# Placing the gate, up and down products of two routed rows in an attention kernel's instruction order

## The chip, the cores and the metric

The kernel runs on one core of a Trainium2 chip. The metric is the device time of one execution in microseconds (us). TensorE (PE in the profile) multiplies matrices, VectorE (DVE), ScalarE (ACT) and GpSimd (POOL) work on elements, and SyncE (SP) issues most of the transfers. Each engine takes its instructions in the order in which they are written.

## The reference

```python
xn = layernorm(x)                       # x: 2048 rows of 640
# attention: 32 heads of 192, keys and values from the last 512 rows of the caches
q = xn @ wq;  p = softmax(q k^T * 192**-0.5);  s = concat(p v) @ wo
# routed part: the two rows with the highest r = xn @ w_r
x_sel = rows of xn at the two positions
y = (silu(x_sel @ w_gate) * (x_sel @ w_up)) @ w_down     # 640 -> 1536 -> 640
y = y * sigmoid(r at the two positions)
g = silu(xn + scatter(y to the two positions))
out = x + s * g
```

The attention is nearly all of the work. The routed part has two rows only, but its result is needed by g for these rows, and it runs inside the attention as a background job.

## The kernel before

**Units and stretches.** A unit n is 128 rows of queries of a pair of heads; there are 256. Units are worked on in stretches of three (the first two stretches have two units). Stretch j starts with the scores of its units and ends with the value products of the units of stretch j-1. From stretch 11 on the order within a stretch is built by a function, `stretch(j)`, as a list of tokens, and the tokens are emitted one after the other. Because the schedule is manual, the order of emission is the order on each engine.

**The order in a stretch** is: S (scores of three units, six matmuls over 128 rows of the contraction and six over the other 64), B.j.0 (background, slot 0), M (six row maxima on DVE, L332), E (exponentials on ACT, L339, two for each unit) with P (transposes of the probabilities on SP, L344) for the first two units, then q (query projections, L303, with their evacuations on ACT, L295), E and P of the third unit, B.j.1, W (output products, L406, evacuated by DVE, L420) with B.j.2 behind the first of them, O (value products of stretch j-1, L358, evacuated by DVE, L373), T (the transpose of their result, L379) and B.j.3. A stretch has two or three q and one or two W, by due times that a planner works out. In the stretches of interest these are: 31 (two q, two W), 36 (two q, one W), 41 (three q, one W) and 48 (two q, two W).

**PSUM.** There are two pools. `ps_p` has six buffers, for the scores (six in a stretch), the W tiles (two for each W) and the first two O tiles of a stretch. `ps_f` has two buffers, for q, for the third O tile, and for the background products `gu_ps` and `y_ps`.

**Background jobs** are put at a unit's stretch and a slot by

```python
def at(n, slot, f):
    bg[st_of[min(n, NU - 1)], slot].append(f)
```

and emitted when the token B.j.slot comes up. The ones of the routed part that matter here are:

- `m_ffn_piece(fb, q)`: ten transfers for each of three blocks fb of 512 columns, which load the gate and up weights into one tile `wgu` (a pool of one buffer, shared with the down weights `wd` and with `y_bc`).
- `m_mul(fb)`: twenty matmuls of the two rows (in 32 columns, in four column groups) with the gate and up weights into `gu_ps` (L576), a tanh on ACT (L580), and two steps on DVE (L581, L582) that give h.
- `m_hT(fb)`: a transpose of h by SP (L588).
- `m_wd_piece(q)`: six transfers of the down weights.
- `m_down`: 48 matmuls of the same kind into `y_ps` (L613), one step on DVE (L616), then five transfers from POOL that bring y to all partitions (L619, L621).
- `m_add(n)` on POOL (L625, L628, L629), which adds y to the routed rows, and `m_tanh(n)` on ACT (L634), which reads the sum.

Of the kernel before, what the change touches and what calls it, by code (L numbers as in the profile page):

```python
# [21 lines left out]
def kernel(ctx, tc, A_x, A_k_cache, A_v_cache, A_wq, A_wo, B_x, B_w_r, B_w_gate, B_w_up, B_w_down, out):  # L22
# [52 lines left out]
    def f_tile(shape, dtype, name):  # L75
        return ps_f.tile(shape, dtype, name=name, tag="f")
# [485 lines left out]
    def m_ffn_piece(fb, q):  # L562
        def f():
            if q == 0:
                M["wgu"] = M["w"].tile([P, 2, DC, 512], BF16, name="wgu", tag="w")
            w, dc = divmod(q, DC)
            src = (B_w_gate, B_w_up)[w].rearrange("(c p) f -> p c f", p=P)
            nc.sync.dma_start(out=M["wgu"][:, w, dc, :], in_=src[:, dc, fb * 512:(fb + 1) * 512])
        return f

    def m_mul(fb):
        def f():
            gu = f_tile([P, 2, P], FP32, "gu_ps")
            for dc in range(DC):
                for c in range(4):
                    nc.tensor.matmul(gu[32 * c:32 * c + 32], lhsT=M["xsT"][:, dc, 0:32], rhs=M["wgu"][:, :, dc, c * P:(c + 1) * P],  # L576
                                     start=(dc == 0), stop=(dc == DC - 1), skip_group_check=True)
            th = M["s"].tile([P, P], FP32, name="th", tag="t2")
            h = M["s"].tile([P, P], BF16, name="h", tag="turned")
            nc.scalar.activation(out=th, in_=gu[:, 0, :], func=ACT.Tanh, scale=0.5)  # L580
            nc.vector.scalar_tensor_tensor(out=th, in0=th, scalar=1.0, in1=gu[:, 0, :], op0=ALU.add, op1=ALU.mult)  # L581
            nc.vector.scalar_tensor_tensor(out=h, in0=th, scalar=0.5, in1=gu[:, 1, :], op0=ALU.mult, op1=ALU.mult)  # L582
            M["h"] = h
        return f

    def m_hT(fb):
        def f():
            nc.sync.dma_start_transpose(out=M["hT"][:, fb * 4:(fb + 1) * 4, :].rearrange("p c t -> p (c t)"), in_=M["h"])  # L588
        return f
# [149 lines left out]
    def at(n, slot, f):  # L739
        bg[st_of[min(n, NU - 1)], slot].append(f)  # L740

    for g in range(2, NG):
        n0 = 32 * g
# [25 lines left out]
    for fb, n0 in enumerate((72, 91, 106)):  # L769
        for q in range(2 * DC):  # L770
            at(n0 + q, 0, m_ffn_piece(fb, q))
        at(n0 + (16, 14, 14)[fb], 3, m_mul(fb))
        at(n0 + (16, 14, 14)[fb], 3, m_hT(fb))
    for q in range(FC // 2):
        at(121 + 3 * q, 0, m_wd_piece(q))
    at(124, 3, m_sig)
    at(141, 2, m_down)
    for n in range(NTB):
        at(147 + 2 * n, 3, m_add(n))
        at(186 + 2 * n, 0, lambda n=n: m_tanh(n))  # L780
# [131 lines left out]
```

## Time and profile before

| what | value |
|---|---|
| median of 3 runs | 792.39 us (791.88 to 793.05) |
| the profiled execution, its own time | 792.56 us |
| its span on the core | 790.8 us |
| granted TensorE clock | 1.00 |
| gate and up products, start | 279.97, 326.32 and 372.68 us |
| down product, start | 432.35 us |
| start of the scores of stretches 31, 36, 41, 48 | 280.63, 326.99, 373.34, 436.91 us |

The span is from the first to the last instruction of the core in one profiled execution, and the time of that execution is a little longer. Rows in order of time give the start and the length in us, the engine, the line, and what is written from what; equal instructions that follow each other are merged, with their count behind x. What stands in brackets is the idle time of the engine before the row and what ended it. SPq is the queue of SP with its DMA issues.

### The profile page before, as it was taken

What the parts mean: (1) busy time and instruction counts of PE and PEld (TensorE: products, weight loads), DVE (VectorE), ACT (ScalarE), POOL (GpSimd) and SP (SyncE); (2) the same over time, 40 slices, a digit from 0 to 9 for tenths busy, and PEclk for the clock granted to TensorE, in tenths of its full rate; (3) what the DMA queues carried; (4) which work ended last, traced back from release to release, by engine and by line L of the source; (5) the groups of instructions that cost most, each with busy time, mean ns of one, the idle gap of its engine ahead of it and who ended that gap; (6) DMA issues with size and microseconds to landing.
All of it is one profiled execution on the core that took longest, in us unless ns stands there. A gap on an engine that the chain in (4) does not pass through costs nothing. (4 is left out here: it accounts for less than half of the span.)

```text
span 790.8 us, 15678 instructions
## 1 busy us (share of the span) xinstructions
PE 782.3 (99%) x5762; PEld 482.9 (61%) x5763; DVE 620.7 (78%) x1238; ACT 479.4 (61%) x1293; POOL 178.9 (23%) x196
## 2 busy tenths in 40 slices
PE   8999999999999999999999999999999999999998
PEld 4556665666655666656666665666566666556666
DVE  6985578988888777777777777777788988777786
ACT  7886765567555656555575556565666865565652
POOL 3220000000010000000000599970000000165966
PEclk9999999999999999999999999999999999999999
DMA  9999998799979999899997999779998899997995
GB/s 249 200 210 197 223 205 144 142 188 192 183 130 216 199 200 216 130 223 204 195 219 140 174 181 196 155 141 176 199 167 144 142 194 183 183 195 150 179 167 142
DMA packets 453901, 143.80 MB, mean 182 GB/s; under 512 B 422382, under 2 KB 453488, under 8 KB 453824
## 3 DMA queue, kind: packets, MB, share of 16 engines
q1 hardware_dynamic: 449376, 138.29, 94.6%
q10 hardware_dynamic: 3760, 2.84, 1.4%
q0 software_dynamic: 688, 1.68, 0.8%
q8 instruction: 45, 0.74, 0.4%
q14 instruction: 32, 0.26, 0.1%
HBM read 39.98 MB, written 2.62 MB: 54 GB/s over the span
## 5 line engine op out<-in xcount | busy, mean ns | idle before, releaser
L339 ACT ACTIVATE pexp<-sc,nm 128x512 bf16<-128x512 f32 x512 | 348.3, 697 | 263.6 <-issue 230.4
L332 DVE TENSOR_REDUCE nm<-sc 128x1 f32<-128x512 f32 x512 | 315.1, 682 | 76.4 <-PE sc L324 76.1
L303 PE MATMUL q_ps<-xnT,wq_p 128*128 128x512 bf16 (+1 forms) x985 | 225.6, 374 | 2.2 <-DMA xnT<-xn 1.0
L406 PE MATMUL w_ps<-wo_g,oT 128*128 128x320 bf16 x1542 | 222.9, 298 | 0.0
L406 PEld LDWEIGHTS <-oT 128*128 128x128 bf16 x1542 | 150.3, 98 | 69.7
L358 PE MATMUL o_ps<-v_sb,pT 128*128 128x192 bf16 x2048 | 185.7, 246 | 0.7 <-DMA pT<-pexp 0.5
L358 PEld LDWEIGHTS <-pT 128*128 128x128 bf16 x2048 | 171.2, 98 | 16.4 <-issue 3.5
L373 DVE TENSOR_TENSOR o_sb<-o_ps,lsum 128x384 bf16<-128x384 f32 x246 | 135.4, 556 | 40.6 <-PE o_ps L358 22.5
L303 PEld LDWEIGHTS <-wq_p 128*128 128x128 bf16 x985 | 89.8, 98 | 123.3 <-issue 34.8
L317 PE MATMUL sc<-kT,qT 128*128 128x512 bf16 x512 | 124.8, 379 | 0.5 <-DVE qT L293 0.5
L420 DVE TENSOR_TENSOR s_acc<-s_acc,w_ps 128x320 f32<-128x320 f32 x192 | 92.6, 484 | 30.7 <-PE w_ps L406 30.6
L339 ACT ACTIVATION_READ_ACCUMULATOR pexp<-sc,nm 128x1 f32 x512 | 110.1, 215 | 0.0
L295 ACT ACTIVATE qT<-q_ps 128x512 bf16<-128x512 f32 (+1 forms) x183 | 100.9, 606 | 2.1 <-PE q_ps L303 2.1
L317 PEld LDWEIGHTS <-qT 128*128 128x128 bf16 x512 | 48.5, 98 | 41.9 <-DVE qT L293 0.7
L324 PE MATMUL sc<-kT,qT 64*128 64x512 bf16 x512 | 70.2, 380 | 0.0
L324 PEld LDWEIGHTS <-qT 64*128 64x128 bf16 x512 | 18.0, 94 | 46.5 <-issue 36.1
L650 POOL TENSOR_TENSOR s_acc<-s_acc,xn 128x640 f32<-128x640 f32 x16 | 22.9, 1434 | 102.2 <-DVE s_acc L420 102.1
L629 POOL TENSOR_TENSOR xn<-xn,yh 128x640 bf16<-128x640 bf16 x32 | 44.6, 1395 | 2.7
L619 POOL DMA_DIRECT2D y_d<-y_sb x4 | 2.2, 546 | 181.2 <-DVE y_sb L616 181.2
L496 POOL DMA_DIRECT2D c_d<-cand x1 | 0.7, 727 | 163.9 <-DVE cand L494 163.9
L651 POOL TENSOR_TENSOR s_acc<-s_acc,x_fin 128x640 f32<-128x640 f32 x16 | 22.4, 1400 | 61.7 <-DVE s_acc L420 54.3
L628 POOL TENSOR_SCALAR yh<-y_bc,oh 128x640 bf16<-128x640 bf16 x32 | 25.7, 802 | 6.0 <-DMA y_bc<-y_d 4.4
(108 smaller groups left out, 227.4 us busy)
## 6 DMA issues: line engine op xcount, KB each, us to landing
wo_g<-in_A_wo_dram SPq DMA_DIRECT2D x15, 480.0 KB, 4.4
wq_p<-in_A_wq_dram SPq DMA_DIRECT2D x14, 480.0 KB, 4.9
k_raw<-in_A_k_cache_dram SPq DMA_DIRECT2D x30, 192.0 KB, 3.4
v_sb<-in_A_v_cache_dram SPq DMA_DIRECT2D x15, 384.0 KB, 4.1
pT<-pexp SPq DMA_TRANSPOSE x256, 3.7
x_fin<-in_A_x_dram SPq DMA_DIRECT2D x16, 160.0 KB, 2.8
wgu<-in_B_w_gate_dram SPq DMA_DIRECT2D x15, 128.0 KB, 2.9
wgu<-in_B_w_up_dram SPq DMA_DIRECT2D x15, 128.0 KB, 3.7
```

Of the source, the lines that this page charges most:

```text
L295: nc.scalar.activation(out=out, in_=in_, func=ACT.Copy, scale=scale)
L303: nc.tensor.matmul(q_ps, lhsT=wq_of[g * PAIRS + pr][:, dc, c * P:(c + 1) * P], rhs=xnT[:, t5 * 4 + lo:t5 * 4 + hi, dc, :], start=(dc == 0) ...
L317: nc.tensor.matmul(sc_of[n][hh], lhsT=qT_of[i][:, 2 * hh, u * P:(u + 1) * P], rhs=kp[:, :, 2 * hh, :], start=True, stop=False)
L324: nc.tensor.matmul(sc_of[n][hh], lhsT=qT_of[i][hs, 1, u * P:(u + 1) * P], rhs=kp[hs, :, 1, :], start=False, stop=True)
L332: nc.vector.tensor_reduce(out=nm_of[j][:, c:c + 1], in_=sc_of[n][hh], axis=AX.X, op=ALU.max, negate=True)
L339: nc.scalar.activation(out=pe_of[n][:, hh, :], in_=sc_of[n][hh], func=ACT.Exp, bias=nm_of[j][:, c:c + 1], scale=1.0, accum_out=l_of[j][:, ...
L358: nc.tensor.matmul(ps[:, hh, :], lhsT=pT_of[n][:, hh, jj, :], rhs=v_sb[:, hh, jj, :], start=(jj == 0), stop=(jj == NJ - 1))
L373: nc.vector.tensor_tensor(out=osb_of[j][:, m], in0=ps, in1=l_of[j][:, 2 * m:2 * m + 2].unsqueeze(2).to_broadcast([P, 2, Dh]), op=ALU.mult)
L406: nc.tensor.matmul(w_ps, lhsT=oT_of[j][:, stretches[j].index(n), c % 3, :], rhs=wo_of[g][:, c, lo:hi], start=(c == 0), stop=(c == CPG - 1))
L420: nc.vector.tensor_tensor(out=acc, in0=acc, in1=w_ps, op=ALU.add)
L628: nc.gpsimd.tensor_scalar(out=yh, in0=M["y_bc"][:, j, :], scalar1=M["oh"][:, n, j:j + 1], scalar2=0.0, op0=ALU.mult, op1=ALU.add)
L629: nc.gpsimd.tensor_tensor(out=xn[:, n, :], in0=xn[:, n, :], in1=yh, op=ALU.add)
```

## The change

The three gate and up products are placed at the unit three units later, which is the next stretch, and in slot 0, behind that stretch's scores, in place of slot 3 at the end of a stretch. The transposes of their results stay in slot 3, and so go to the end of that next stretch. The down product is placed in slot 0 of stretch 48 in place of slot 2 (between the two W) of stretch 47. What is computed does not change.

```diff
     for fb, n0 in enumerate((72, 91, 106)):
         for q in range(2 * DC):
             at(n0 + q, 0, m_ffn_piece(fb, q))
-        at(n0 + (16, 14, 14)[fb], 3, m_mul(fb))
-        at(n0 + (16, 14, 14)[fb], 3, m_hT(fb))
+        at(n0 + (16, 14, 14)[fb] + 3, 0, m_mul(fb))
+        at(n0 + (16, 14, 14)[fb] + 3, 3, m_hT(fb))
     for q in range(FC // 2):
         at(121 + 3 * q, 0, m_wd_piece(q))
     at(124, 3, m_sig)
-    at(141, 2, m_down)
+    at(144, 0, m_down)
```

## The prediction

> **What bounds the kernel now.** I read the page's first lines, then who TensorE (PE) waits for, then the instructions in order of time around the four places that the change touches.
>
> ```profile
> span 790.8 us, 15678 instructions
> ...
> PE 782.3 (99%) x5762; PEld 482.9 (61%) x5763; DVE 620.7 (78%) x1238; ACT 479.4 (61%) x1293; POOL 178.9 (23%) x196
> ```
> ```profile
> PE q_ps L303 <- DMA xnT<-xn: 1.0, 1, 1.0
> ...
> PE sc L317 <- DVE qT L293: 0.5, 1, 0.5
> ```
>
> TensorE is busy 782.3 of 790.8 us, and its recorded waits are single ones of about 1 us. So any time that TensorE gets more work, or is made to wait in mid-run, is added to the end; the other engines matter only through what they make TensorE wait for. Now one plain stretch (stretch 30, from 270.32, with the first gate/up product at its tail) on TensorE alone. Columns: start, us, engine, line, what.
>
> ```profile
> 270.32 1.46 PE L317 MATMUL sc<-kT,qT 128*128 128x512 bf16 x6
> 271.71 0.82 PE L324 MATMUL sc<-kT,qT 64*128 64x512 bf16 x6
> 272.47 2.33 PE L303 MATMUL q_ps<-xnT,wq_p 128*128 128x512 bf16 x10
> 274.64 3.42 PE L406 MATMUL w_ps<-wo_g,oT 128*128 128x320 bf16 x24
> 277.90 2.14 PE L358 MATMUL o_ps<-v_sb,pT 128*128 128x192 bf16 x24
> 279.97 0.73 PE L576 MATMUL gu_ps<-wgu,xsT 128*32 128x256 bf16 x20
> 280.63 1.47 PE L317 MATMUL sc<-kT,qT 128*128 128x512 bf16 x6
> ...
> 290.20 1.46 PE L317 MATMUL sc<-kT,qT 128*128 128x512 bf16 x6
> ```
>
> I call the start of a stretch's scores S. Then q follows at S+2.15 (272.47-270.32), the output products w at S+4.32, the o products at S+7.58. A stretch with two w and no extra product is 290.20-280.63 = 9.57 long; this one is 280.63-270.32 = 10.31, so the product costs TensorE 0.74 where it stands. What hangs on the scores on the two evacuating engines, in the same stretch:
>
> ```profile
> 272.14 3.68 DVE L332 TENSOR_REDUCE nm<-sc 128x1 f32<-128x512 f32 x6 [1.06 <-PE sc L324]
> ...
> 272.91 0.69 ACT L339 ACTIVATE pexp<-sc,nm 128x512 bf16<-128x512 f32 x1 [3.41 <-issue]
> ...
> 273.50 0.19 ACT L339 ACTIVATION_READ_ACCUMULATOR pexp<-sc,nm 128x1 f32 x1
> ...
> 275.58 1.09 ACT L295 ACTIVATE qT<-q_ps 128x512 bf16<-128x512 f32 x2
> ...
> 277.10 0.24 ACT L339 ACTIVATION_READ_ACCUMULATOR pexp<-sc,nm 128x1 f32 x1
> ...
> 277.77 0.24 ACT L339 ACTIVATION_READ_ACCUMULATOR pexp<-sc,nm 128x1 f32 x1
> ...
> 280.75 0.28 ACT L580 ACTIVATE th<-gu_ps 128x128 f32<-128x128 f32 x1 [2.74 <-PE gu_ps L576]
> 281.06 0.29 DVE L581 SCALAR_TENSOR_TENSOR th<-th,gu_ps 128x128 f32<-128x128 f32 x1 [0.43 <-ACT th L580]
> 281.38 0.29 DVE L582 SCALAR_TENSOR_TENSOR h<-th,gu_ps 128x128 bf16<-128x128 f32 x1
> ```
>
> The six row maxima (L332) start at S+1.82; each exponential follows its maximum, and frees one score tile. When the exponential gives its tile back is read at another place: its accumulator read ends at 430.15+0.20 = 430.35, and the transpose that waits for it is issued at 430.37. So I count a tile as free at the end of that read.
>
> ```profile
> 430.15 0.20 ACT L339 ACTIVATION_READ_ACCUMULATOR pexp<-sc,nm 128x1 f32 x1
> ...
> 430.37 5.37 SPq L344 DMA_TRANSPOSE pT<-pexp  x3
> ```
>
> In the plain stretch the first score tile is free at 273.69 (S+3.37), the fifth at 277.34 (S+7.02), the sixth at 278.01 (S+7.69). Pool ps_p has six buffers and the scores take all six, so w, at S+4.32, has 0.95 to spare on the first tile; the first two o products (S+7.58 and 0.66 later, 24 matmuls in 1.98) have 0.56 and 0.55 on the fifth and sixth. These small margins decide the case.
>
> **The product behind the scores.** In slot 0 the emission order is scores, product, row maxima. On TensorE the product takes S+2.15, where q stood. It shifts everything behind it by 0.66 (280.63-279.97) rather than 0.74: the 0.08 of getting into it from the o products is not paid, since a change of shape follows the scores anyway (their second pass is 64*128). I keep -0.1 to +0.25 as bounds of the start behind the 64-row pass, which no row shows; 0 is taken, because q, also of another shape, starts there at once.
>
> The Trainium skill, TensorEngine Tiling (Array Packing), section Key Properties, says that changing the tiling mode drains the array; the change has one mode change less for each product, so by this rule alone it is a gain. The trace agrees on the size of one entry, 0.08.
>
> But the product also brings one tanh on ACT and two steps on DVE, and both engines take them in the order written. From the product's start to the end of h is 281.38+0.29-279.97 = 1.70, and the next step follows 0.03 later. Before, that ran while the next scores were being made, in the 1.06 that DVE waits for scores anyway. Now the six maxima are queued behind it: they start at S+2.15+1.73 = S+3.88 in place of S+1.82. **Maxima, exponentials, q evacuations and the freeing of all six tiles come 2.06 later, while TensorE's own work is only 0.66 later.** The margins above are smaller than the difference of 1.40.
>
> *Stretch 31 (two q, two w).* w would start at 4.98, the first tile is free at 3.37+2.06 = 5.43: wait 0.45. o then at 5.43+3.26 = 8.69, the fifth tile at 9.08: wait 0.39. Second o at 9.74, sixth tile 9.75. Next scores at 9.75+1.32 = 11.07, against 9.57+0.74 = 10.31 for the same work before: **+0.76**.
>
> *Stretch 36 (two q, one w).*
>
> ```profile
> 326.99 1.47 PE L317 MATMUL sc<-kT,qT 128*128 128x512 bf16 x6
> ...
> 332.94 2.14 PE L358 MATMUL o_ps<-v_sb,pT 128*128 128x192 bf16 x24
> 334.92 1.46 PE L317 MATMUL sc<-kT,qT 128*128 128x512 bf16 x6
> ```
>
> Length 7.93, o at S+5.95, that is 1.63 behind w. With one w the o products reuse the third and fourth tiles, and the next scores the fifth and sixth. w at 5.43, o at 7.06, next scores at 9.04; their second matmul, 0.23 later (1.39 for six), needs the sixth tile at 9.75: a wait of 0.48. Effective end 9.52 against 7.93+0.74 = 8.67: **+0.85**.
>
> *Stretch 41 (three q, one w).*
>
> ```profile
> 373.34 1.47 PE L317 MATMUL sc<-kT,qT 128*128 128x512 bf16 x6
> ...
> 378.61 1.09 ACT L295 ACTIVATE qT<-q_ps 128x512 bf16<-128x512 f32 x2
> ...
> 379.29 1.24 PE L303 MATMUL q_ps<-xnT,wq_p 128*128 128x512 bf16 x5
> ...
> 380.37 2.14 PE L358 MATMUL o_ps<-v_sb,pT 128*128 128x192 bf16 x24
> ...
> 382.35 1.46 PE L317 MATMUL sc<-kT,qT 128*128 128x512 bf16 x6
> ```
>
> The third q, at S+5.95, needs one of the two buffers of ps_f, which the first q evacuation frees at S+5.27+0.55 = 5.82 (margin 0.13). That evacuation stands behind four exponentials: 5.82+2.06 = 7.88. The third q starts there, and 382.35-379.29 = 3.06 later come the next scores: 10.94 against 9.01+0.74 = 9.75: **+1.19**, the largest term.
>
> *Stretch 48 (down product, two q, two w).*
>
> ```profile
> 426.31 1.46 PE L317 MATMUL sc<-kT,qT 128*128 128x512 bf16 x6
> ...
> 432.35 1.01 PE L613 MATMUL y_ps<-wd,hT 128*32 128x160 bf16 x48
> ...
> 433.29 1.80 PE L406 MATMUL w_ps<-wo_g,oT 128*128 128x320 bf16 x12
> 433.42 0.38 DVE L616 TENSOR_SCALAR y_sb<-y_ps,sgp 128x160 bf16<-128x160 f32 x1 [0.47 <-PE y_ps L613]
> ...
> 436.91 1.46 PE L317 MATMUL sc<-kT,qT 128*128 128x512 bf16 x6
> ```
>
> Before, it costs 10.60-9.57 = 1.03; behind the scores 0.94 (433.29-432.35). Its one DVE step ends 1.45 behind its start, no ACT step: the maxima start at 2.15+1.48 = 3.63, 1.81 late. w at 5.26 finds its tile (5.18). o at 8.52 waits for the fifth tile, 8.83; the second o at 9.49 for the sixth, 9.50. Next scores 10.82 against 10.60: **+0.22**.
>
> **What moves at no cost.**
>
> ```profile
> 328.81 1.18 SPq L588 DMA_TRANSPOSE hT<-h  x1
> 330.09 1.48 SPq L568 DMA_DIRECT2D wgu<-in_B_w_gate_dram x3
> ```
> ```profile
> L629 POOL TENSOR_TENSOR xn<-xn,yh x32: 1392/1394/1400, 445.8 to 528.2; 128x640 bf16<-128x640 bf16 x32
> ```
> ```profile
> L634 ACT ACTIVATE tz<-xn x16: 736/778/790, 561.0 to 654.7; 128x640 f32<-128x640 bf16 x16
> ```
>
> SP: the three hT transposes (1.18 each) go one stretch back, behind that stretch's pT and oT; the first reader of hT is the down product, more than 50 us later. The next weight pieces share the tile that the product reads, so they now wait on SP until the product ends, S+2.15+0.73 = 2.88. They were issued at 330.09 = S+3.10, and without hT ahead could go 1.18 sooner: a wait of about 1 us. Queued behind it is the first pT, whose exponentials are free only at 6 us: hidden. POOL: the down product starts near 436.91-1.03+2.80+2.15 = 440.8 in place of 432.35 (2.80 are the first three terms), so the routed additions end near 538 in place of 528.2+1.4 = 529.6; the first tanh that reads them is at 561.0: hidden, with 23 us left.
>
> **Sum.** 0.76+0.85+1.19+0.22 = 3.02. The profiled execution took 792.56 (span 790.8 and 1.76 around it), so 795.58; that execution lies 0.17 above the median of the runs, 792.39, against which I give **795.4**.
>
> **Rivals.**
>
> *Not slower: only the mode change counts.* If DVE took the maxima ahead of the product's two steps, nothing would be late and the change would save 3 x 0.08 + 0.09 = 0.33: 792.1. It decides where the maxima are less than 0.79 late at the third q (0.66+0.13) and less than 1.61 at w (0.66+0.95). For it: the tiling rule above, and that all work is merely reordered. Against: h's steps are written ahead of the maxima, and 2.06 is beyond both points. 0.13.
>
> *Half the price: tiles come back in another order.* If w and o may take whichever tile is free, only the waits that no order avoids remain: w in stretches 31 and 36 (10.67-10.31 = 0.36, 9.04-8.67 = 0.37), the third q (1.19), and -0.09 for the down product: 1.83, so 794.2. For it: no row shows which buffer a tile got. Against: a pool that hands out in turn is the simple case, and its margins of 0.56 and 0.55 are met by the trace without a wait. 0.16.
>
> *Dearer: late transposes.* The last pT of these stretches is issued at 9.75 in place of about 7.7; three take 5.37 to issue. If that once held an o product for one issue (1.8) the time would be 797.2. Against: the o that needs it stands some 8 us later. 0.05.
>
> **How the numbers follow.** The forecast has 0.66. About 0.2% (1.6 us) is what a measurement of this kernel can tell from no change. The range takes in the forecast, the cheaper rival and the bounds of the product's start (-0.1 to +0.25 over four places, so -0.4 to +1.0), with a little for the scatter of the runs: 793.5 to 796.8; it leaves out the first rival and the dearer one. Same: most of the first rival and a part of the cheaper one that falls under 1.6, 0.15; faster 0.04, as even the whole mode-change gain is a fifth of what could be told; slower 0.81.
>
> **What would show it.** In the changed trace the L332 groups of stretches 31, 36 and 41 start about 3.9 behind their scores, and that of 48 about 3.6; TensorE shows gaps ahead of L406, L358, or (third q) L303 with ACT as releaser; score-to-score distances of about 11.07, 9.5, 10.94 and 10.82; stretches 30, 35, 40 and 47 shrink to 9.57, 7.92, 9.56 and 9.57. The forecast is wrong if the maxima start near S+2 there, or if they are late and the distances are still 10.2, 8.6, 9.7 and 10.5.

## The result, and the profile after

The changed kernel takes 792.96 us (median of 14 runs, 792.37 to 794.31) against 792.33 us before (14 runs, 790.72 to 793.13) in the same comparison. The ratio is 1.0016, with a 95% interval of 1.0009 to 1.0023: slower by 1.3 us (0.7 to 1.8). The two medians by themselves differ by only 0.63 us, so the time tells the direction and little of the size; in what follows, microseconds behind a ratio are the ratio times the time before. The forecast was +3.0 us. The direction is right; the size is a little under half by the time, and a little over half by the trace below.

The page of the changed kernel says nothing of it. The span even reads 790.6, shorter than before, since one execution's opening (stretches 0 to 10) differs by more than the change: the scores of stretch 30 start at 268.59 in place of 270.32. So I compare from score start to score start, from the stretch that loses the product to the end of the one that takes it.

```profile
span 790.6 us, 15674 instructions
...
PE 781.6 (99%) x5763; PEld 482.8 (61%) x5763; DVE 619.9 (78%) x1238; ACT 479.3 (61%) x1293; POOL 178.6 (23%) x196
```

| stretches | forecast | before | after | difference |
|---|---|---|---|---|
| 30 and 31 (first gate/up) | +0.76 | 19.88 | 20.15 | +0.27 |
| 35 and 36 (second) | +0.85 | 16.61 | 16.89 | +0.28 |
| 40 and 41 (third) | +1.19 | 19.32 | 20.46 | +1.14 |
| 47 and 48 (down) | +0.22 | 20.16 | 20.05 | -0.11 |
| sum | +3.02 | | | +1.58 |

The sum of 1.58 lies in the interval of the timed runs, and the regular stretches behind 48 have the same lengths in both traces. Stretch 31 after the change, TensorE in order of time (start, us, engine, line, what, and in brackets the idle time with what ended it):

```profile
278.15 1.46 PE L317 MATMUL sc<-kT,qT 128*128 128x512 bf16 x6
279.54 0.82 PE L324 MATMUL sc<-kT,qT 64*128 64x512 bf16 x6
280.29 0.73 PE L576 MATMUL gu_ps<-wgu,xsT 128*32 128x256 bf16 x20
280.95 2.35 PE L303 MATMUL q_ps<-xnT,wq_p 128*128 128x512 bf16 x10
283.50 3.42 PE L406 MATMUL w_ps<-wo_g,oT 128*128 128x320 bf16 x24 [0.20 <-ACT pexp L339]
286.76 2.14 PE L358 MATMUL o_ps<-v_sb,pT 128*128 128x192 bf16 x24
288.74 1.46 PE L317 MATMUL sc<-kT,qT 128*128 128x512 bf16 x6
```

The product starts at S+2.14 and w waits for an exponential, as forecast. (The bracket counts only 0.20 of it: w starts at S+5.35, where it would start at S+4.98 without the wait.) But o follows w after its usual 3.26, and the next scores follow o after 1.98: no second wait. DVE and ACT beside it:

```profile
281.07 0.28 ACT L580 ACTIVATE th<-gu_ps 128x128 f32<-128x128 f32 x1 [4.79 <-PE gu_ps L576]
281.38 0.29 DVE L581 SCALAR_TENSOR_TENSOR th<-th,gu_ps 128x128 f32<-128x128 f32 x1 [2.48 <-ACT th L580]
...
281.70 0.29 DVE L582 SCALAR_TENSOR_TENSOR h<-th,gu_ps 128x128 bf16<-128x128 f32 x1
281.91 3.67 DVE L332 TENSOR_REDUCE nm<-sc 128x1 f32<-128x512 f32 x6
...
282.68 0.69 ACT L339 ACTIVATE pexp<-sc,nm 128x512 bf16<-128x512 f32 x1 [1.33 <-DVE nm L332]
...
283.26 0.19 ACT L339 ACTIVATION_READ_ACCUMULATOR pexp<-sc,nm 128x1 f32 x1
...
286.87 0.24 ACT L339 ACTIVATION_READ_ACCUMULATOR pexp<-sc,nm 128x1 f32 x1
```

DVE idles 2.48 ahead of the product's steps, and the maxima start at S+3.76 (forecast 3.88, before 1.82): the hold is there. The first score tile is free at 283.45, and w starts 0.05 later. The fifth is free at 286.87+0.24 = 287.11, but o started at 286.76: **it did not wait for that tile, so it has another one.** Which one, no row shows. Stretch 36 shows the same, with one wait at w and then the usual 3.61 to the next scores:

```profile
324.78 1.46 PE L317 MATMUL sc<-kT,qT 128*128 128x512 bf16 x6
...
330.13 1.79 PE L406 MATMUL w_ps<-wo_g,oT 128*128 128x320 bf16 x12 [0.20 <-ACT pexp L339]
...
333.74 1.46 PE L317 MATMUL sc<-kT,qT 128*128 128x512 bf16 x6
```

Stretch 41 goes as forecast: the third q waits for the first q evacuation, and starts at S+7.85 (forecast 7.88). w is late here too, at S+5.36, but the third q's wait ends later and covers it.

```profile
371.40 1.46 PE L317 MATMUL sc<-kT,qT 128*128 128x512 bf16 x6
...
376.76 1.79 PE L406 MATMUL w_ps<-wo_g,oT 128*128 128x320 bf16 x12
...
378.60 1.09 ACT L295 ACTIVATE qT<-q_ps 128x512 bf16<-128x512 f32 x2
...
379.25 1.24 PE L303 MATMUL q_ps<-xnT,wq_p 128*128 128x512 bf16 x5 [0.70 <-ACT qT L295]
...
382.31 1.46 PE L317 MATMUL sc<-kT,qT 128*128 128x512 bf16 x6
```

Stretch 48 has late maxima too (S+3.51) and no wait at all. There the move is a small gain.

```profile
435.82 1.46 PE L317 MATMUL sc<-kT,qT 128*128 128x512 bf16 x6
...
437.96 1.01 PE L613 MATMUL y_ps<-wd,hT 128*32 128x160 bf16 x48
...
439.33 3.67 DVE L332 TENSOR_REDUCE nm<-sc 128x1 f32<-128x512 f32 x6
...
441.08 3.42 PE L406 MATMUL w_ps<-wo_g,oT 128*128 128x320 bf16 x24
...
446.32 1.46 PE L317 MATMUL sc<-kT,qT 128*128 128x512 bf16 x6
```

### The profile page after: what moved, and what is told of

The parts are those of the page before. It is cut to its first block, busy times and chain, and to the rows that moved or that the text cites. A ratio compares the mean times of both kernels' runs of the same rounds, so it can differ in the third digit from the quotient of the medians.

```text
span 790.6 us, 15674 instructions
## 1 busy us (share of the span) xinstructions
PE 781.6 (99%) x5763; PEld 482.8 (61%) x5763; DVE 619.9 (78%) x1238; ACT 479.3 (61%) x1293; POOL 178.6 (23%) x196
```

## The experiments

The theory after the result: what costs is lateness of the maxima beyond two margins (the first score tile at w, the first q evacuation at the third q), both counted against TensorE's own work, which is late as well; and the o products get a tile that is free already. The main rival is the forecast's reading, tiles strictly in turn. Each expectation was on record before its run.

### The down product alone

```diff
-    at(141, 2, m_down)
+    at(144, 0, m_down)
```

> Only the down product moves behind the scores of stretch 48; the three gate/up products stand where they stood before. Theory (what costs is the wait on score tiles that are freed late, and the pool hands the o products a tile that is already free): stretches 47 and 48 together are 0.1 us shorter than before (20.05 against 20.16), the time is the same within what can be told. Rival (tiles are handed out strictly in turn, as the forecast had it): o waits for the fifth and sixth score tile, stretches 47 and 48 together 0.22 us longer.

Measured: 790.87 against 791.18, ratio 0.9999 (0.9990 to 1.0008), the same. In the trace stretches 47 and 48 are 9.55 and 10.50 long, -0.11 against before. This fits the theory and not the rival; the time by itself could not have told it.

### The third product one stretch earlier

```diff
-        at(n0 + (16, 14, 14)[fb] + 3, 0, m_mul(fb))
-        at(n0 + (16, 14, 14)[fb] + 3, 3, m_hT(fb))
+        at(n0 + (19, 17, 12)[fb], 0, m_mul(fb))
+        at(n0 + (19, 17, 12)[fb], 3, m_hT(fb))
```

> The changed kernel, but with the third gate/up product one stretch earlier, behind the scores of stretch 40 (two q) in place of 41 (three q). Theory (the third q of stretch 41, which waits for a q evacuation queued behind the late exponentials, is 1.14 us of the loss): the wait at the third q is gone, stretch 40 loses 0.28 us by the wait at w like stretches 31 and 36, and the sum is 3 x 0.28 - 0.11 = +0.73 us over before in place of +1.59. Rival (each of the moved products costs the same wherever it lands): the loss stays near +1.6 us.

Measured: ratio 1.0013 (1.0004 to 1.0022), +1.0 us, which tells it neither from +0.7 nor from +1.6. The trace does. TensorE in stretch 40, and the third q of stretch 41, now without a wait:

```profile
363.20 1.46 PE L317 MATMUL sc<-kT,qT 128*128 128x512 bf16 x6
...
368.56 3.42 PE L406 MATMUL w_ps<-wo_g,oT 128*128 128x320 bf16 x24 [0.20 <-ACT pexp L339]
...
373.80 1.46 PE L317 MATMUL sc<-kT,qT 128*128 128x512 bf16 x6
...
379.74 1.24 PE L303 MATMUL q_ps<-xnT,wq_p 128*128 128x512 bf16 x5
```

Stretch 40 is 10.60 long and 41 is 9.00, +0.28 together in place of +1.14. All four places sum to +0.71 (expected 0.73).

### The product's steps left out

```diff
-            nc.scalar.activation(out=th, in_=gu[:, 0, :], func=ACT.Tanh, scale=0.5)
-            nc.vector.scalar_tensor_tensor(out=th, ...)
-            nc.vector.scalar_tensor_tensor(out=h, ...)
+            nc.gpsimd.memset(h, 0.0)
```

> The changed kernel without the tanh and the two DVE steps of the gate/up products (h is set to zeros by GpSimd instead, so that part of the computation is left out); the matmuls, the transfers and the transposes stay. Theory (the row maxima are late because they are queued behind these steps): maxima start at S+1.8 in stretches 31, 36 and 41, no wait at w or at the third q, and the time is 0.3 us under before. Rival (the place of the matmuls behind the 64-row pass is itself dear, by a change of shape or by the two ps_f buffers): the loss of about 1.6 us stays.

Measured: 790.57 against 791.18, ratio 0.9994 (0.9985 to 1.0003). In the trace the maxima of stretch 31, whose scores start at 278.52, are where they were before the change, S+1.82:

```profile
280.34 3.68 DVE L332 TENSOR_REDUCE nm<-sc 128x1 f32<-128x512 f32 x6 [1.06 <-PE sc L324]
```

Nothing waits, and the four places are 0.11, 0.11, 0.10 and 0.11 shorter than before, -0.43 (expected -0.3). So the matmuls cost no more behind the 64-row pass than at the end of a stretch, rather 0.1 less; the loss is made by the three small steps.

### The steps behind two maxima

```diff
-        out_ += ["M.%d.%d" % (n, hh) for n in us for hh in range(2)]
+        out_ += ["M.%d.%d" % (us[0], hh) for hh in range(2)] + ["B.%d.4" % j]
+        out_ += ["M.%d.%d" % (n, hh) for n in us[1:] for hh in range(2)]
...
+        at(n0 + (16, 14, 14)[fb] + 3, 4, m_h)
```

Here `m_h` holds the two DVE steps, which are taken out of `m_mul`.

> The changed kernel with the two DVE steps of each gate/up product put behind the first two row maxima of the stretch in place of ahead of all six; the matmuls and the tanh stay behind the scores. Theory (only the lateness of the first tiles and of the q evacuation counts, against margins of 0.95 and 0.13): the first exponential is about 0.65 late (behind the tanh) and the others about 0.7, just as late as TensorE itself (0.66), no wait at w or at the third q, and the time is 0.3 us under before, which the trace can show and the time hardly. Rival (any delay of the evacuating engines comes through to the end): 0.3 to 0.7 us lost in each of three stretches, +1 to +2 us.

Measured: 790.95 against 791.18, ratio 0.9998 (0.9989 to 1.0007). DVE in stretch 31 (scores at 278.28), and w on time at S+4.99 without a wait:

```profile
280.10 1.29 DVE L332 TENSOR_REDUCE nm<-sc 128x1 f32<-128x512 f32 x2 [1.06 <-PE sc L324]
...
281.51 0.29 DVE L586 SCALAR_TENSOR_TENSOR th<-th,gu_ps 128x128 f32<-128x128 f32 x1
281.84 0.29 DVE L587 SCALAR_TENSOR_TENSOR h<-th,gu_ps 128x128 bf16<-128x128 f32 x1
...
282.04 2.48 DVE L332 TENSOR_REDUCE nm<-sc 128x1 f32<-128x512 f32 x4
...
283.27 3.42 PE L406 MATMUL w_ps<-wo_g,oT 128*128 128x320 bf16 x24
```

The four places give -0.10, -0.09, -0.01 and -0.11: -0.31 against before (expected -0.3). Stretch 41 keeps 0.09 of its loss: its third q starts at S+6.69, and at S+6.60 in the run without the steps. This version does the whole computation, and in the four places it is shorter than both kernels; in time it cannot be told from the kernel before.

### One maximum twice, in the stretches with three q

```diff
+        out_ += ["M.%d.0" % us[0]] * (len(qs) == 3)
         out_ += ["M.%d.%d" % (n, hh) for n in us for hh in range(2)]
```

> The kernel before, with the first row maximum taken twice in each of the 18 stretches with three q (13 to 81): everything behind it on DVE and ACT is 0.60 us later, and TensorE's own work does not change. Theory (the third q has a margin of 0.13 on the first q evacuation): 0.47 lost in each, 18 x 0.47 = +8.5 us. Rivals: any lateness counts in full, 18 x 0.60 = +10.8 us; or it is covered, as DVE is busy only 78 per cent, 0.

Measured: 804.27 against 791.25, ratio 1.0165 (1.0148 to 1.0182), +13.0 us: more than the theory gave, and more than the lateness in full. The trace of one such stretch tells why:

```profile
303.97 4.41 DVE L332 TENSOR_REDUCE nm<-sc 128x1 f32<-128x512 f32 x7 [1.06 <-PE sc L324]
...
308.13 1.09 ACT L295 ACTIVATE qT<-q_ps 128x512 bf16<-128x512 f32 x2
...
308.79 1.24 PE L303 MATMUL q_ps<-xnT,wq_p 128*128 128x512 bf16 x5 [0.53 <-ACT qT L295]
```

Seven maxima take 4.41 where six take 3.68, so the repeated one adds 0.73, not 0.60. The stretch is 9.69 long in place of 9.00: 0.69 of 0.73 comes through, a margin of 0.04 in place of 0.13. The third q starts 0.66 behind the start of the pair of evacuations, and before the change 379.29-378.61 = 0.68: it stood at its limit already. I had taken half of the pair's 1.09 for the first. 18 x 0.69 = 12.4 of the 13.0. With the true dose of 0.73, the rival of lateness in full gives 18 x 0.73 = 13.1, so this run does not decide against it; the next one does.

### One maximum twice, in the stretches with two q

The same edit with `len(qs) == 2`.

> The kernel before, with the first row maximum taken twice in each of the 56 stretches with two q between 11 and 84: 0.60 us later there. Theory (w has 0.95 to spare on the first score tile and o gets a tile that is free): nothing lost, 0 to +1 us. Rivals: tiles strictly in turn, o has 0.56 and 0.55 to spare, about 0.05 lost in each, +2 to +3 us; any lateness in full, 56 x 0.60 = +33.6 us.

Measured: 793.11 against 791.25, ratio 1.0028 (1.0017 to 1.0039), +2.2 us: more than the theory gave, and within the 2 to 3 of the rival of tiles in turn. By the trace, which sums to 1.8 from stretch 11 on, 53 of the 56 stretches keep their length, though the dose is 0.73 here too. So lateness does not count in full. Stretch 47 is 0.60 longer, where the down product, still at its old place, needs a buffer of ps_f:

```profile
PE y_ps L613 <- ACT qT L295: 0.5, 1, 0.5
```

Four more stretches are 0.18 to 0.49 longer without a recorded wait: 20 and 28, and 21 and 69, which have three q and no maximum more. In 20, 21 and 69 the trace shows DVE reach the maxima late, at S+2.18, S+2.35 and S+2.15: a background step of 0.8 (L473 or L637), which had room before the maxima until now, is still running then. In stretch 20 this lateness of 0.36 and the dose of 0.73 together exceed the margin at w, and w starts at S+4.50 in place of S+4.31; in 21 and 69 the third q, with next to no margin, is late. In stretch 28 the scores themselves take 1.70 in place of 1.46; what holds them stays open. No loss repeats over the stretches, as tiles in turn would have it.

### One maximum three times, in the stretches with two q

The same edit with `2 * (len(qs) == 2)`.

> The kernel before, with the first row maximum taken three times in each of the 56 stretches with two q: 1.20 us later there. Theory: w waits 1.20 - 0.95 = 0.25, with 0.05 for the signal 0.30, and nothing else waits, 56 x 0.25 to 0.30 = +14 to +17 us. Rival (tiles strictly in turn): o or the next scores wait too, 0.64 to 0.73 in each, about +38 us. Rival (in full): +67 us.

Measured: 824.55 against 791.25, ratio 1.0423 (1.0405 to 1.0440), +33.5 us, where the theory gave 14 to 17. TensorE's waits, and DVE in one stretch:

```profile
PE w_ps L406 <- ACT pexp L339: 21.5, 55, 0.7
```
```profile
330.33 5.13 DVE L332 TENSOR_REDUCE nm<-sc 128x1 f32<-128x512 f32 x8 [1.06 <-PE sc L324]
```

Eight maxima take 5.13, 1.45 more than six. Most of these stretches are 0.55 longer (10.11 for 9.56, 8.47 for 7.92), so the margin at w is 1.45-0.55 = 0.90; 55 x 0.55 = 30.3. The only repeated wait is w's. The expectation missed in the dose, 1.45 and not 1.20, not in the mechanism: with 1.45, tiles in turn would cost about 1.45-0.56 = 0.89 in each. The total by itself looked more like the rival's 38.

### The buffers strictly in turn, before and after

Six tags (names) with one buffer each, taken in turn, in place of one tag with six buffers, in both kernels:

```diff
-    ps_p = pool("ps_p", 6, space=bass.MemoryType.PSUM)
+    ps_p = pool("ps_p", 1, space=bass.MemoryType.PSUM)
+    turn_of = [0]
...
-        return ps_p.tile(shape, dtype, name=name, tag="p")
+        turn_of[0] = (turn_of[0] + 1) % 6
+        return ps_p.tile(shape, dtype, name=name, tag="p%d" % turn_of[0])
```

> The kernel before, with the six buffers of ps_p handed out strictly in turn, as the forecast had assumed. Both theories: the margins of 0.56 and 0.55 at the o products are met, no wait in the regular stretches, lengths of 9.55, 7.92 and 9.00 as before; the same time, but for the irregular opening (stretches 0 to 10), whose tile order also changes.

> The changed kernel with the six buffers of ps_p handed out strictly in turn; to be read against the kernel before with the same buffers. Theory (the forecast failed at its assumption on the buffers, and nowhere else by much): stretches 31, 36, 41 and 48 are 11.0, 9.45, 10.9 and 10.75 long, 0.7 + 0.8 + 1.15 + 0.15 = +2.8 us in place of +1.6. Rival (o and the next scores have other slack that the forecast overlooked, whatever buffer they get): lengths of 10.6, 8.96, 10.9 and 10.5 as in the changed kernel, +1.6 us.

Measured: 795.64 for the kernel before and 798.20 for the changed one (ratios to the kernel before 1.0046, 1.0033 to 1.0059, and 1.0085, 1.0070 to 1.0099). The first is 3.6 us slower; all of its recorded waits of TensorE, among them single ones of up to 2.1 for exponentials, lie in the first 100 us, the irregular opening, and there is none behind it, as expected. What counts is the difference of the two, +2.56 us by the medians and 3.1 by the ratios; their intervals are too wide to tell 1.6 from 2.8, so the trace decides. The changed kernel with buffers in turn (lines are two higher), stretch 31 and the first scores behind stretch 36:

```profile
283.29 1.46 PE L319 MATMUL sc<-kT,qT 128*128 128x512 bf16 x6
...
288.64 3.42 PE L408 MATMUL w_ps<-wo_g,oT 128*128 128x320 bf16 x24 [0.20 <-ACT pexp L341]
292.30 2.15 PE L360 MATMUL o_ps<-v_sb,pT 128*128 128x192 bf16 x24 [0.23 <-ACT pexp L341]
294.28 1.46 PE L319 MATMUL sc<-kT,qT 128*128 128x512 bf16 x6
```
```profile
339.33 0.38 PE L319 MATMUL sc<-kT,qT 128*128 128x512 bf16 x1
340.00 1.24 PE L319 MATMUL sc<-kT,qT 128*128 128x512 bf16 x5 [0.29 <-ACT pexp L341]
```

The second wait, at o, and the wait of the second score are there as the prediction described them. With the 0.45 that this score costs counted to stretch 36, as the prediction did, the stretches are 10.99, 9.47, 10.91 and 10.75 long (expected 11.0, 9.45, 10.9 and 10.75); against the kernel before with the same buffers the four places give 0.67+0.78+1.15+0.15 = +2.75.

## Why the prediction was right or wrong

**Right:** the hold. The row maxima are queued behind the product's tanh and two steps and start 1.94 late (forecast 2.06); the run without these steps has neither the lateness nor the loss. Right too: TensorE is shifted by 0.66 by the product itself, w and the third q are the two places that wait, stretch 41 is the dearest (1.14, forecast 1.19), and SP and POOL hide what moves there: the last routed addition now starts at 531.7 (sooner than the forecast's end near 538) and the first tanh that reads them at 560.8.

**Wrong: the step "with one w the o products reuse the third and fourth tiles", and its like for two w, the fifth and sixth.** That the tiles of ps_p are handed out in turn was assumed, not read from a row. The changed kernel's o starts before the fifth tile is free. With the buffers forced in turn the forecast's waits appear, and 2.75 of its 3.02 with them. The terms it mis-sized are stretch 31 (0.76, measured 0.27), stretch 36 (0.85, measured 0.28) and stretch 48 (+0.22, measured -0.11). The prediction had this as its second rival, 1.83 in all, with a chance of 0.16; the trace gives 1.58. The measured time, 792.39 x 1.0016 = 793.7 (median 792.96), is at the low end of the range of 793.5 to 796.8: what reaches so far down is the allowance for this rival, not the worked sum of 795.4. Its reason against that rival, margins that the trace meets without a wait, was none: an order with more room meets them as well.

**Off in size only:** the maxima start 0.12 earlier than summed, because the first of them overlaps the end of h (281.91 against 281.70+0.29 = 281.99); so w waits about 0.1 less. The margin at the third q is 0.04 and not 0.13. These two errors cancel in stretch 41.

**The rule of the Trainium skill** (TensorEngine Tiling (Array Packing), section Key Properties), that a change of tiling mode drains the array, agrees in sign with the runs where no step is held up: each product then saves 0.10 to 0.11, against the 0.08 and 0.09 of the forecast. The Trainium skill gives no price there, and that the drain is what is saved no run shows by itself. By this rule alone the change would be a gain; it is not, because 0.11 is a tenth of what the held steps cost in stretch 41.

## What to carry to other kernels

When a product is moved on the bound engine, follow its small evacuating steps on the other engines first: what is queued behind them, and how much later that may be before the bound engine notices. Such margins differ by place (0.90 at w, 0.04 at the third q), so a gate and up product costs 0.27 or 0.28 us in two stretches and 1.14 in another, the down product with its single small step nothing, and putting the DVE steps behind the first two maxima keeps most of the gain. Which buffer an operation gets is a fact of the program, to be read from starts and releases and not to be assumed.

## What the runs showed that I had not expected

A row maximum taken again on the same tile, into the same column, adds 0.73 us, where six on different tiles follow each other every 0.60 (3.68 for six, 4.41 for seven, 5.13 for eight). Whether the tile or the column makes the difference, no run shows. And two q evacuations in a row take 1.09 together, but the q that waits for the first starts 0.65 to 0.66 behind its start, not at half of the pair.
